# Two half-height matmuls side by side in TensorE's rows: the second passes of a 64-row tile in a GEGLU layer's gate and up

## The chip, the cores and the metric

The kernel runs on one core of one Trainium2 chip. The metric is the device time of one execution in microseconds, the median over several runs. The matrix engine (TensorE, PE in the profile) multiplies a stationary operand, loaded into its array of 128 rows by 128 columns by a weight load (PEld), with a moving operand, and adds the result to a bank of PSUM. VectorE is DVE, ScalarE is ACT, GpSimd is POOL, SyncE is SP.

## The reference

All arrays are float32; S = 2048 tokens, D = 448, F = 1792.

```python
def ref(x, dft_seq_re, dft_seq_im, dft_hid_re, dft_hid_im, w_gate, w_up, w_down):
    xn = layernorm(x)                                  # 2048 x 448, no scale or shift
    a, b = xn @ dft_hid_re.T, xn @ dft_hid_im.T        # Fourier transform over the hidden axis
    s = dft_seq_re @ a - dft_seq_im @ b                # and over the tokens, real part
    g = silu((gelu(xn @ w_gate) * (xn @ w_up)) @ w_down)
    return x + s * g
```

The change concerns `xn @ w_gate` and `xn @ w_up`, together 2048 x 448 by 448 x 3584.

## The kernel before, in words

**Precision.** Each float32 operand is split into a high part (rounded to the type fp32r of the matrix engine, by ScalarE) and a low part (the rest, by VectorE). A product is three passes over the array: high by high, high by low and low by high; low by low is left out. `three` (line 468) issues these.

**The stages.** After layernorm, transposes and the first two tiles of F in the ordinary way (`gu_mm`, line 394), 24 units of gate and up in seven products follow (function `strassen`, line 480), six groups of four, from about 72 to 397 us. Then come the hidden transform (`hid_mm`, line 985) and the transform over the tokens, also in seven products (lines 1174 and 1177).

**One unit** takes one tile of F (128 columns of gate and 128 of up) and one pair of token blocks (512 tokens each, c and e). Gate and up for both blocks are a 2 x 2 block product, made from seven products with sums of the operands by Winograd's scheme. The contraction of 448 is cut into four tiles of 128, 128, 128 and 64 rows; two by two these are the halves of the inner axis, so each of the seven products has two tiles. Four PSUM banks x1 to x4 hold the results. Sums of the weights are made by GpSimd (`sums_s`), sums of the tokens by `combine`, once; `t` and `v` are the token sums split into high and low, `hl(c, k)` the plain tokens.

**The tile of 64 rows.** Tokens of that tile are stored twice, in rows 0 to 63 and again in rows 64 to 127. Three weight tiles, x4, x2 and x3 (the first 384 columns of a weight slot), meet it. They hold the high part of the 64 weight rows in rows 0 to 63 and the low part in rows 64 to 127; line 360 makes that low part. So one pass over 128 rows adds high by high and low by high together, and a second pass with the tokens' low part adds high by low (and low by low). `two` (line 475, matmuls at line 478) issues these two passes, three times a unit: for x1, for x3 and for x4.

**The order.** It is written out by hand: the program order of each engine is the order of the calls in `strassen`, with four slots `dn` (each issues one output tile of the down product, six matmuls at line 448, and its copy out of PSUM by ScalarE, line 455) and four slots `preps` (weights of a later unit: line 354 on ScalarE, lines 356 and 360 on VectorE). `late` is the end of the unit before. Around the change the order on TensorE is: a12 and x2 into x1, a22 and x3 into x3, a down tile, s4 and x4 into x4, a down tile. ScalarE takes the gelu of x1 (line 519), VectorE adds x3 (line 523) and multiplies (line 524), ScalarE makes the high part of the result (line 526) and VectorE the low one (line 528).

Of the kernel before, what the change touches and what calls it, by code (L numbers as in the profile page):

```python
# [8 lines left out]
F32 = mybir.dt.float32  # L9
FR = mybir.dt.float32r  # L10
AF = mybir.ActivationFunctionType
ALU = mybir.AluOpType

P = 128
# [31 lines left out]
def fnet_geglu(ctx: ExitStack, tc: tile.TileContext, x, ca, ct, cp, et, wgu, wd, out):  # L46
# [13 lines left out]
    nc = tc.nc  # L60
# [31 lines left out]
    def tmp(i):  # L92
        return a_t[:, 512 * i : 512 * i + 512]
# [7 lines left out]
    def xk(c, k, lo=0):  # L101
        at = k if c % 2 == 0 else (0, 2, 1, 3)[k]
        return a_x[c][:, 2048 * lo + 512 * at :][:, :512]
# [17 lines left out]
    def bank(i, name):  # L121
        return psum.tile([P, 512], F32, name=name, tag=f"b{i}")
# [12 lines left out]
    def mm_tile(name):  # L135
        return in_turn("mm", name)
# [165 lines left out]
    def slot(i):  # L302
        return a_w[:, 3200 * i :][:, :3200]
# [43 lines left out]
    def prep_s(i, raw):  # L347

        w = slot(i)
        hw = w[:, :1792]  # L350
        steps = []

        def part_(a, b):
            nc.scalar.activation(hw[:, a:b], raw[:, P + a : P + b], AF.Copy)  # L354
            lo = max(a, 384)
            nc.vector.tensor_sub(  # L356
                w[:, 1408 + lo : 1408 + b], raw[:, P + lo : P + b], hw[:, lo:b].bitcast(F32)
            )
            if a == 0:
                nc.vector.tensor_sub(  # L360
                    hw[64:, :384], raw[64:, P : P + 384], hw[64:, :384].bitcast(F32)
                )

        names = "x4 x2 x3 s1 a11 a12 a22 b11 r1 s3 s2 s4 r3 r2".split()
        parts = {}
        for n, name in enumerate(names):
            parts[name] = [w[:, n * P : (n + 1) * P]]
            if n > 2:
                parts[name].append(w[:, 1408 + n * P : 1408 + (n + 1) * P])
        return parts, [lambda: part_(0, 896), lambda: part_(896, 1792)]  # L370
# [38 lines left out]
    def new_hs(f, c):  # L409
        hs_of[f, c] = hs_tile()  # L410
        return hs_of[f, c]
# [56 lines left out]
    def three(ps, a, b, first=False):  # L468

        for n, (i, j) in enumerate(((0, 0), (0, 1), (1, 0))):  # L470
            nc.tensor.matmul(  # L471
                ps, a[i], b[j], start=first and n == 0, stop=n == 2, skip_group_check=True
            )

    def two(ps, a, b):

        for xt in b:
            nc.tensor.matmul(ps, a[0], xt, start=False, stop=True, skip_group_check=True)  # L478

    def strassen(f, p, w, late, dn, preps):  # L480


        c, e = 2 * p, 2 * p + 1
        m, u, g1, c21 = [tmp(i) for i in ((0, 1, 2, 3), (2, 3, 0, 1))[units_n[0] % 2]]
        units_n[0] += 1

        def hl(c, k):
            return xk(c, k), xk(c, k, 1)

        t, v = t_hl[p]  # L490

        def bank(i):
            return mm_tile(f"x{i}_{f}_{p}")

        x1 = bank(1)
        three(x1, w["a11"], hl(c, 0), True)
        three(x1, w["b11"], hl(c, 2))
        nc.scalar.activation(m, x1, AF.Copy)
        late[0]()
        x2 = bank(2)  # L500
        three(x2, w["s2"], t[1], True)
        three(x2, w["r2"], v[1])
        nc.vector.tensor_add(u, m, x2)
        late[1]()
        dn[0]()
        preps[0]()
        x3 = bank(3)
        three(x3, w["s3"], t[2], True)
        three(x3, w["r3"], v[2])
        nc.vector.tensor_add(m, u, x3)  # L510
        x4 = bank(4)
        three(x4, w["s1"], t[0], True)
        three(x4, w["r1"], v[0])
        nc.vector.tensor_add(m, m, x4)
        preps[1]()
        dn[1]()
        three(x1, w["a12"], hl(c, 1))
        two(x1, w["x2"], hl(c, 3))
        nc.scalar.activation(g1, x1, AF.Gelu_apprx_tanh)
        preps[2]()  # L520
        three(x3, w["a22"], t[3])
        two(x3, w["x3"], v[3])
        nc.vector.tensor_add(c21, u, x3)
        nc.vector.tensor_mul(g1, g1, c21)  # L524
        hs = new_hs(f, c)
        nc.scalar.activation(hs[:, 0], g1, AF.Copy)  # L526
        dn[2]()
        nc.vector.tensor_sub(hs[:, 1], g1, hs[:, 0])
        preps[3]()
        three(x4, w["s4"], hl(e, 1))  # L530
        two(x4, w["x4"], hl(e, 3))
        nc.vector.tensor_add(u, u, x4)
        nc.scalar.activation(u, u, AF.Gelu_apprx_tanh)
        dn[3]()

        def late0():
            nc.vector.tensor_mul(u, u, m)
            late0.hs = new_hs(f, e)
            nc.scalar.activation(late0.hs[:, 0], u, AF.Copy)

        def late1():
            nc.vector.tensor_sub(late0.hs[:, 1], u, late0.hs[:, 0])

        return late0, late1
# [4 lines left out]
    with tc.manual_schedule():  # L549
# [294 lines left out]
        for gi in range(1, len(GROUPS)):  # L844
# [7 lines left out]
            for bi, (i, p) in enumerate(zip((0, 1, 1, 0), sides)):  # L852
# [63 lines left out]
                if gi == 1 and bi < 2:  # L916
                    dn = [nop, send, nop, send]
                run = [lambda q=q: [f() for f in q] for q in preps]
                late = strassen(grp[i], p, ws[i], late, dn, run)
                sum_step(4 * gi + bi - 4)  # L920
                if bi % 2:
# [52 lines left out]
        def hid_mm(k):  # L974
            c, kk = divmod(k, 4)
            sl = slice(kk * P, (kk + 1) * P)
            ps = []
            for r in range(2):
                p = (mm_tile if k < 2 else in_turn8)(f"ab{k}_{r}")
                xh, xl = [[xk(c, b, lo)[:, sl] for b in range(4)] for lo in range(2)]  # L980
                mm = [(xh[b], e_at[b][r]) for b in range(4)]
                mm += [(xh[b], e_at[b][2 + r]) for b in range(3)]
                mm += [(xl[b], e_at[b][r]) for b in range(4)]
                for n, (a, b) in enumerate(mm):
                    nc.tensor.matmul(p[:, :D], a, b, start=n == 0, stop=n == len(mm) - 1)  # L985
                ps.append(p[:, :D])
            return ps
# [101 lines left out]
        for k in [*range(14), 15, 14]:  # L1089
            ps = hid_mm(k)  # L1090
# [24 lines left out]
            for c, at, v in ((2, 3, (a_st, 0)), (3, 4, None), (0, 4, None), (1, 5, (a_st, 1))):  # L1115
                if k == at:
                    v, i = v or (x0, int(c == 0))
# [145 lines left out]
        def gather(ps):  # L1263

            p = {q: v[:, :D].rearrange("p (w d) -> p w d", w=2) for q, v in ps.items()}
            c11, c12, c21, c22 = [cv[t][:, :, s] for t in range(2) for s in range(2)]
            nc.scalar.activation(c11, p[1], AF.Copy)
            return [
                lambda: nc.vector.tensor_sub(c12, c11, p[6]),
                lambda: nc.vector.tensor_add(c11, c11, p[2]),  # L1270
                lambda: nc.vector.tensor_add(c21, c12, p[7]),
                lambda: nc.vector.tensor_sub(c12, c12, p[5]),
                lambda: nc.vector.tensor_sub(c22, p[5], c21),
                lambda: nc.vector.tensor_add(c12, c12, p[3]),
                lambda: nc.vector.tensor_sub(c21, p[4], c21),
            ]
# [15 lines left out]
        for m, (j, k) in enumerate(units):  # L1292
            u = m % UN
            if u == 0:
                ps = {q: bank(banks[i], f"p{q}_{j}") for i, q in enumerate(PRODUCTS)}
            if u < NS:
                if j < NK // 2 - 1 or u < NS - 2:
                    seven(m, ps)
                for i, at in enumerate(LOAD_AT if j < NK // 2 - 1 else LAST_AT):
# [5 lines left out]
                    a, b = [v.rearrange("p (b d) -> p b d", d=D) for v in (TS[n], td[n])]  # L1305
                    a, b = a[:, PARTS[h]], b[:, PARTS[h]]
# [13 lines left out]
            elif u == NS - 1:  # L1320
                todo = gather(ps)
# [10 lines left out]
            elif u == NS + 1:  # L1332
                prep_c(m + 3)
                c = cs[1][0]
# [75 lines left out]
```

## Time and profile before

| | |
|---|---|
| time, median of 3 runs | 769.71 us (769.7 to 770.01) |
| profiled execution | 769.68 us |
| its span, first to last instruction | 767.8 us |
| TensorE busy, matmuls / weight loads | 761.8 / 686.6 us (99% / 89% of the span) |
| VectorE / ScalarE / GpSimd busy | 544.8 / 366.2 / 180.1 us |
| matmuls in all | 4054 |
| granted TensorE clock | 1.00 |

Times are microseconds unless marked ns. A row of the profile names the line of the program, the engine, the operation, what it writes and reads (out<-in, buffer numbers left out, so x1 to x4 are all "x"), the shape, and for TensorE the part of the array that it uses (128*128). Matmuls are pipelined and their ends are modelled: one lasts longer than the distance to its successor's start. The chain of waits is followed back from the last instruction; the chain in order of time gives each piece the time until the next piece starts. L12 is line 12.

### The profile page before, as it was taken

The numbers are of one execution on the slowest core, as the hardware profiler recorded it, in microseconds if no ns is written. First come the engines' busy times: TensorE is split into PE (matmuls) and PEld (weight loads), VectorE is DVE, ScalarE is ACT, GpSimd is POOL, SyncE is SP. The second block draws the span as 40 slices with busy tenths as digits, with TensorE's granted clock in tenths as the row PEclk, the third lists the DMA queues.
The fourth block names the chain that finished last, engine by engine and source line by source line (L and its number), as shares of the span: only waits on it lengthen the run. The fifth ranks groups of instructions, "written<-read, shape, count | busy, mean of one in ns | idle before, by whom it ended". The sixth has DMA issues, their size and how long they took to land.

```text
span 767.8 us, 11360 instructions
## 1 busy us (share of the span) xinstructions
PE 761.8 (99%) x4054; PEld 686.6 (89%) x4054; DVE 544.8 (71%) x947; ACT 366.2 (48%) x546; POOL 180.1 (23%) x303
## 2 busy tenths in 40 slices
PE   8999999999999999999999999999999999999998
PEld 7988888888888888888889999999999999999997
DVE  7889877555556556456452776888888797979787
ACT  5875554444444344344444585544444444434341
POOL 2204043430501512501011001223232322323130
PEclk9999999999999999999999999999999999999999
DMA  8234458994959968875979981959696969788794
GB/s 297 91 120 150 145 203 176 258 186 105 266 105 254 269 117 221 176 156 86 260 215 244 371 340 54 311 181 333 216 355 191 355 205 333 222 301 264 260 299 166
DMA packets 61513, 170.04 MB, mean 221 GB/s; under 512 B 7440, under 2 KB 40080, under 8 KB 60560
## 3 DMA queue, kind: packets, MB, share of 16 engines
q0 software_dynamic: 13728, 61.02, 35.0%
q1 hardware_dynamic: 34272, 82.48, 30.5%
q10 hardware_dynamic: 13456, 25.81, 9.2%
q8 instruction: 32, 0.52, 0.3%
q14 instruction: 25, 0.20, 0.1%
HBM read 127.21 MB, written 70.91 MB: 258 GB/s over the span
## 4 chain that ended last, share of the span: by engine, by line
PE 98%; DVE 1%; issue 0%; ACT 0%; DVEq 0%
PE x L471 24%; PE p L1174 22%; PE po L448 18%; PE p L1177 10%; PE ab L985 9%; PE x L478 4%; PE gu L394 4%; PE py L1189 1%; PE py L1191 1%; PE py L1190 1%; PE gu L597 1%; PE pt L198 1%; PE warm L571 1%; PE p L1207 0%; DVE st L155 0%
## 5 line engine op out<-in xcount | busy, mean ns | idle before, releaser
L471 PE MATMUL x<-xt,w 128*128 128x512 f32 x480 | 149.4, 392 | 0.0
L471 PEld LDWEIGHTS x<-xt,w 128*128 128x128 f32 x480 | 90.1, 188 | 16.1 <-DVE tmp L510 0.4
L455 ACT ACTIVATE po_out<-po 128x448 f32<-128x448 f32 x112 | 60.2, 537 | 81.6 <-PE po L448 80.0
L448 PE MATMUL po<-wd0h,hs 128*128 128x448 f32 x256 | 81.7, 366 | 0.0
L460 POOL DMA_DIRECT2D gs<-po_out x24 | 21.4, 893 | 218.8 <-ACT po_out L455 218.7
L985 PE MATMUL ab<-e,xt 128*128 128x448 f32 x288 | 68.8, 365 | 0.0
L448 PE MATMUL po<-wd,hs 128*128 128x448 f32 x288 | 66.0, 365 | 0.0
L471 PE MATMUL x<-t_v,w 128*128 128x512 f32 x216 | 60.7, 389 | 0.0
L448 PEld LDWEIGHTS po<-wd,hs 128*128 128x128 f32 x288 | 54.1, 188 | 6.7
L985 PEld LDWEIGHTS ab<-e,xt 128*128 128x128 f32 x288 | 54.1, 188 | 4.3
L448 PEld LDWEIGHTS po<-wd0h,hs 128*128 128x128 f32 x256 | 48.1, 188 | 4.9
L471 PEld LDWEIGHTS x<-t_v,w 128*128 128x128 f32 x216 | 40.5, 188 | 8.7
L1065 POOL DMA_DIRECT2D raw<-sums x45 | 24.8, 553 | 94.9 <-DVE xt L143 55.5
L448 PE MATMUL po<-wd0l,hs 128*128 128x448 f32 x128 | 46.9, 367 | 0.0
L142 ACT ACTIVATE e<-raw 128x896 fp32r<-128x896 f32 (+1 forms) x30 | 27.7, 923 | 38.6 <-DVE raw L1072 25.8
L526 ACT ACTIVATE hs<-tmp 128x512 fp32r<-128x512 f32 x24 | 15.2, 635 | 54.6 <-DVE tmp L524 54.6
L471 PE MATMUL x<-t_lo,w 128*128 128x512 f32 x96 | 37.4, 389 | 0.0
L142 ACT ACTIVATE e<-tmp 128x896 fp32r<-128x896 f32 (+1 forms) x22 | 19.8, 898 | 35.3 <-DVE tmp L1072 26.6
L1174 PE MATMUL p<-t_v,wd0l 128*128 128x448 f32 x112 | 36.4, 374 | 0.0
L1174 PE MATMUL p<-w,e 128*128 128x448 f32 x112 | 36.4, 374 | 0.0
L1065 POOL DMA_DIRECT2D tmp<-sums x39 | 21.5, 552 | 61.2 <-DVE xt L143 38.5
L356 DVE TENSOR_TENSOR w<-raw,w 128x512 fp32r<-128x512 f32 (+1 forms) x24 | 21.3, 889 | 18.3 <-ACT w L354 18.3
(373 smaller groups left out, 2019.1 us busy)
## 6 DMA issues: line engine op xcount, KB each, us to landing
gs<-po_out POOLq DMA_DIRECT2D x24, 896.0 KB, 8.4
sums<-ca SPq DMA_DIRECT2D x16, 896.0 KB, 10.8
sums<-ca POOLq DMA_DIRECT2D x16, 896.0 KB, 14.5
t_v<-td ACTq DMA_DIRECT2D x24, 448.0 KB, 5.8
w<-td ACTq DMA_DIRECT2D x24, 448.0 KB, 8.4
raw<-ct SPq DMA_DIRECT2D x45, 192.0 KB, 4.3
raw<-wgu SPq DMA_DIRECT2D x12, 640.0 KB, 5.5
tmp<-ct SPq DMA_DIRECT2D x39, 192.0 KB, 4.7
```

The source lines that it names most:

```text
L142: nc.scalar.activation(h, src, AF.Copy)
L356: nc.vector.tensor_sub(w[:, 1408 + lo : 1408 + b], raw[:, P + lo : P + b], hw[:, lo:b].bitcast(F32))
L394: nc.tensor.matmul(ps[:, cols], a, xt[:, cols], start=n == 0, stop=n == len(mm) - 1)
L448: nc.tensor.matmul(po[:, :D], hs[:, a, kk * P : (kk + 1) * P], wdn[b][:, i], start=n == 0, stop=n == 5,)
L455: nc.scalar.activation(out_[0][:, kk], po[:, :D], AF.Copy)
L460: nc.gpsimd.dma_start(gv[:, 4 * c : 4 * c + 4], out_[0], accum_op=ALU.add)
L471: nc.tensor.matmul(ps, a[i], b[j], start=first and n == 0, stop=n == 2, skip_group_check=True)
L478: nc.tensor.matmul(ps, a[0], xt, start=False, stop=True, skip_group_check=True)
L985: nc.tensor.matmul(p[:, :D], a, b, start=n == 0, stop=n == len(mm) - 1)
L1065: nc.gpsimd.dma_start(v[:, 4 * P : 6 * P], sums[j][:, KS.index(k)])
L1174: nc.tensor.matmul(ps[q][:, :D], h, v, start=u % UN == 0, stop=False, skip_group_check=True)
L1177: nc.tensor.matmul(ps[q][:, :HD], l, v[:, :HD], start=False, stop=u % UN == NS - 1, skip_group_check=True,)
```

## The change

Three things change. In `strassen`, the `two` of x1 and that of x3 issue only their first pass. Their second passes are issued together behind x3's, by a new function `beside`: each contracts over 64 rows only, x1's in rows 0 to 63 of the array and x3's in rows 64 to 127, each to its own bank. The gelu of x1 follows the pair and, on ScalarE and in the order of the calls, comes behind `preps[2]`. So that x3's high weights lie in rows 64 to 127, the weight tile x3 has its halves swapped: the low part goes to rows 0 to 63, and one subtraction (64 x 384) becomes two (64 x 256 and 64 x 128). The product low by low, which the second passes of x1 and x3 added along the way, is no longer added there. x4 keeps both its passes.

```diff
@@ prep_s
             if a == 0:
-                nc.vector.tensor_sub(
-                    hw[64:, :384], raw[64:, P : P + 384], hw[64:, :384].bitcast(F32)
-                )
+                for r, e0, e1 in ((slice(64, P), 0, 256), (slice(0, 64), 256, 384)):
+                    nc.vector.tensor_sub(
+                        hw[r, e0:e1], raw[r, P + e0 : P + e1], hw[r, e0:e1].bitcast(F32)
+                    )
@@ behind two
+    def beside(*todo):
+        for (ps, a, b), at in zip(todo, (0, 64)):
+            r = slice(at, at + 64)
+            nc.tensor.matmul(
+                ps, a[0][r], b[1][r], start=False, stop=True, skip_group_check=True,
+                tile_position=(at, 0),
+            )
@@ strassen
         three(x1, w["a12"], hl(c, 1))
-        two(x1, w["x2"], hl(c, 3))
-        nc.scalar.activation(g1, x1, AF.Gelu_apprx_tanh)
+        two(x1, w["x2"], hl(c, 3)[:1])
         preps[2]()
         three(x3, w["a22"], t[3])
-        two(x3, w["x3"], v[3])
+        two(x3, w["x3"], v[3][:1])
+        beside((x1, w["x2"], hl(c, 3)), (x3, w["x3"], v[3]))
+        nc.scalar.activation(g1, x1, AF.Gelu_apprx_tanh)
         nc.vector.tensor_add(c21, u, x3)
         nc.vector.tensor_mul(g1, g1, c21)
```

TensorE's program order in one unit (the tile of F number 5, first pair of token blocks), from the second use of x1 to the down tile behind x3; x1 and x3 are the banks, xt0 and xt1 plain tokens of the two blocks, t_lo and t_v0 token sums, w the weights, po2 the down tile. Before:

```order
L471 MATMUL x1_5_0_1434<-xt0_66,w_73 128x512 x3
L478 MATMUL x1_5_0_1434<-xt0_66,w_73 128x512 x2
L471 MATMUL x3_5_0_1461<-xt1_67,w_73 128x512
L471 MATMUL x3_5_0_1461<-t_lo_728,w_73 128x512
L471 MATMUL x3_5_0_1461<-xt1_67,w_73 128x512
L478 MATMUL x3_5_0_1461<-t_v0_699,w_73 128x512 x2
L448 MATMUL po2_2_2_1501<-wd0h_76,hs1_80 128x448
```

And now, with the new line 487:

```order
L473 MATMUL x1_5_0_1438<-xt0_66,w_73 128x512 x3
L480 MATMUL x1_5_0_1438<-xt0_66,w_73 128x512
L473 MATMUL x3_5_0_1465<-xt1_67,w_73 128x512
L473 MATMUL x3_5_0_1465<-t_lo_729,w_73 128x512
L473 MATMUL x3_5_0_1465<-xt1_67,w_73 128x512
L480 MATMUL x3_5_0_1465<-t_v0_700,w_73 128x512
L487 MATMUL x1_5_0_1438<-xt0_66,w_73 128x512
L487 MATMUL x3_5_0_1465<-t_v0_700,w_73 128x512
L450 MATMUL po2_2_2_1505<-wd0h_76,hs1_80 128x448
```

One second pass each has gone from x1 and x3, and two matmuls of 64 rows (the row shows the output's shape, 128x512) stand ahead of the down tile.

ScalarE's order in a unit that prepares weights (tile of F number 4, second pair; po1 are down tiles, raw1 the loaded weights, w the prepared ones, tmp the working tiles). Before:

```order
L455 ACTIVATE po_out_82<-po1_2_1_1271 128x448
L519 ACTIVATE tmp_81<-x1_4_1_1225 128x512
L354 ACTIVATE w_73<-raw1_75 128x896
L526 ACTIVATE hs1_80<-tmp_81 128x512
L455 ACTIVATE po_out_82<-po1_2_2_1295 128x448
```

And now:

```order
L457 ACTIVATE po_out_82<-po1_2_1_1275 128x448
L354 ACTIVATE w_73<-raw1_75 128x896
L535 ACTIVATE tmp_81<-x1_4_1_1228 128x512
L539 ACTIVATE hs1_80<-tmp_81 128x512
L457 ACTIVATE po_out_82<-po1_2_2_1299 128x448
```

The gelu of x1 (L519, now L535) has moved behind the copy of the weights (L354).

## The prediction

> **What bounds the kernel now.** I read four views in this order: the page's busy times, its chain of waits, the engines' busy time in the stage that the change touches, and the waits of that stage.
>
> The page's sections 1 and 4 first:
>
> ```profile
> PE 761.8 (99%) x4054; PEld 686.6 (89%) x4054; DVE 544.8 (71%) x947; ACT 366.2 (48%) x546; POOL 180.1 (23%) x303
> PE 98%; DVE 1%; issue 0%; ACT 0%; DVEq 0%
> PE x L471 24%; PE p L1174 22%; PE po L448 18%; PE p L1177 10%; PE ab L985 9%; PE x L478 4%; PE gu L394 4%; PE py L1189 1%; PE py L1191 1%; PE py L1190 1%; PE gu L597 1%; PE pt L198 1%; PE warm L571 1%; PE p L1207 0%; DVE st L155 0%
> ```
>
> TensorE's matmul stream is 98% of the chain that ended last. The lines of gate and up in seven products are L471 (24%) and L478 (4%, the two passes of the 64-row tile). A page's share is an average, so the stage itself, cut in three (columns: stretch, then PE, PEld, DVE, ACT, POOL busy, granted clock, DMA share, GB/s), and its only TensorE wait:
>
> ```profile
> 70.00:180.00 110.00, 110.00 (x501) 93.74 (x500) 75.96 (x107) 50.82 (x89) 30.57 (x52) 1.00 0.70 189
> 180.00:290.00 110.00, 110.00 (x505) 94.49 (x504) 62.96 (x87) 47.28 (x83) 30.66 (x54) 1.00 0.81 193
> 290.00:397.00 107.00, 107.00 (x491) 91.92 (x491) 58.88 (x86) 47.33 (x82) 20.43 (x32) 1.00 0.78 186
> PEld x L471 <- DVE tmp L510: 0.4, 1, 0.4
> ```
>
> From 70 to 397 us TensorE never pauses, at full clock, and waits for another engine 0.4 us in all. What is taken off its stream there is taken off the time, and what is put on it is added. The other engines are idle for a third or more of the stage.
>
> The lengths of the passes come from the chain in order of time (start, length, line, instructions) in one such unit:
>
> ```profile
> 167.69 2.74 PE x L471 x12
> 170.43 1.21 PE po L448 x6
> 171.64 0.70 PE x L471 x3
> 172.34 0.46 PE x L478 x2
> 172.80 0.68 PE x L471 x3
> 173.48 0.45 PE x L478 x2
> 173.93 1.21 PE po L448 x6
> 175.14 0.70 PE x L471 x3
> 175.84 0.46 PE x L478 x2
> ```
>
> A pass over 512 columns occupies the stream 2.74/12 = 228 ns, one over 448 columns 1.21/6 = 202 ns. The difference gives 0.416 ns a column, so 213 ns for 512 columns and about 15 ns a pass that doesn't depend on the columns.
>
> **The change part by part.** The last chain shows three pairs of L478 in a unit; two of them lose their second pass. How many units there are, and how long a pass and its weight load last when they stand alone (minimum, median, maximum ns), is in the rows of L478:
>
> ```profile
> L478 PEld LDWEIGHTS x<-xt,w x96: 187/188/188, 78.9 to 396.1; 128*128 128x128 f32 x96
> L478 PE MATMUL x<-xt,w x96: 388/389/393, 79.2 to 396.3; 128*128 128x512 f32 x96
> L478 PE MATMUL x<-t_v,w x48: 389/389/397, 80.3 to 393.9; 128*128 128x512 f32 x48
> ```
>
> 96 + 48 = 144 passes, six a unit, 24 units. *Removed:* two passes a unit, 2 x 228.3 = 456.7 ns. *Added:* two matmuls of 64 rows over 512 columns. If they run side by side, they cost one pass and a second start: 228.3 + 15.4 = 243.7 ns. (The lower bound of the second start is 0, the upper one a whole pass, 228 ns, if they don't run side by side; I take the 15 ns as the only part of a pass that two instructions in different rows cannot share.) That alone is 213.0 ns a unit, 24 x 213.0 = 5.11 us: 769.68 - 5.11 = 764.6 us.
>
> *The two changes of the array's shape.* Every matmul in this trace is of shape 128*128, so what it costs to go to half-row tiles and back, 48 times, no row shows. It decides the sign: at 213 ns a unit for both, the gain is gone. From below, the nearest row is another change of what the array does, between transposes and products, early in the program:
>
> ```profile
> 33.65 0.44 PE pt L198 x4
> 34.09 1.23 PE po L448 x6
> 35.31 0.44 PE pt L198 x4
> 20.61 0.87 PE pt L198 x8
> ```
>
> Eight transposes in a row take 0.87 us, 109 ns each, so four 0.435; four between products take 0.44. Going in and out costs some 5 ns: lower bound 0. From above: a pass lasts 389 ns from start to end and the next starts after 228, so 161 ns of it lie beside its successor. If the array must have finished all of it, each change costs 161 ns, and if in addition no weight load may run ahead, its 188 ns too. With the second tile's weights loaded 109 ns behind the first's (a transposition, one weight load each, passes every 109 ns), that makes 228 + 109 + 2 x (161 + 188) = 1035 ns a unit in place of 457: +13.9 us, 783.6 us, the upper bound.
>
> The value I take stands between these. A weight load lasts 188 ns but one passes every 109, so 79 ns of it is a run-up that overlaps its predecessor. I assume the same run-up for a matmul: of the 161 ns, 79 are on the way to the array and can overlap, and 161 - 79 = 82 are in the array and behind it. Going in, the full-height pass has to leave: 82 ns. Coming out, a tile of half the rows leaves in half of that: 41 ns. Sum 123 ns a unit. It is nearer to the transposes' row than to the upper one, because only what is in the array needs its shape. Net: 213 - 123 = 90 ns a unit, 24 x 90 = 2.2 us.
>
> On this the Trainium skill speaks against the change: TensorEngine Tiling (Array Packing), Tiling Modes, says that a change of the tiling mode drains the TensorE, without a length. TensorE: Matmul & The Clock Gate, Single matmul latency, puts what a lone matmul takes beyond its columns at 398 cycles at 2.4 GHz, an estimate of 166 ns; with that at each change the sum would be 24 x (332 - 213) = +2.9 us, 772.5 us. The trace's 161 ns agrees with that figure; no row here shows a drain.
>
> *Weights' halves (L360).* One VectorE subtraction of 64x384 becomes two, 64x256 and 64x128, in 12 weight tiles. The rows:
>
> ```profile
> L360 DVE TENSOR_TENSOR w<-raw,w 64x384 fp32r<-64x384 f32 x12 | 6.7, 556 | 0.4
> L356 DVE TENSOR_TENSOR w<-raw,w 128x512 fp32r<-128x512 f32 x12 | 8.2, 686 | 0.7 <-ACT w L354 0.7
> L356 DVE TENSOR_TENSOR w<-raw,w 128x896 fp32r<-128x896 f32 x12 | 13.1, 1091 | 17.7 <-ACT w L354 17.6
> ```
>
> (1091 - 686)/384 = 1.05 ns a column and some 145 ns fixed: the second instruction adds about 0.14 us, 1.7 us in all on VectorE. It is hidden, since VectorE idles in the same unit, 1.96 us of it right behind (timeline of VectorE and ScalarE, idle time in brackets):
>
> ```profile
> 171.79 0.56 DVE L360 TENSOR_TENSOR w<-raw,w 64x384 fp32r<-64x384 f32 x1
> 172.83 0.60 ACT L519 ACTIVATE tmp<-x 128x512 f32<-128x512 f32 x1 [0.61 <-PE x L478]
> 173.33 0.94 ACT L354 ACTIVATE w<-raw 128x896 fp32r<-128x896 f32 x1
> 174.30 1.09 DVE L356 TENSOR_TENSOR w<-raw,w 128x896 fp32r<-128x896 f32 x1 [1.96 <-ACT w L354]
> 175.31 0.68 DVE L523 TENSOR_TENSOR tmp<-tmp,x 128x512 f32<-128x512 f32 x1
> ```
>
> Without that cover it would cost 1.7 us.
>
> *The gelu (L519) moves behind the pair.* Here x1 would be ready at about 173.8 instead of 172.8, and its 0.60 us end by 174.5 at the latest. Behind it on ScalarE stand the copy of L526, which needs L524 and hence L523, at 175.31 + 0.68 anyway, and before it the weight copy L354, which now goes first and is done earlier, so L356 too. TensorE needs x1's bank again in the next unit, after two products of down (1.21 us each) and five passes (1.14 us): not before 177 us. Cost 0; if the 2.5 us of slack were gone, the next unit's first pass would wait. No DMA is issued elsewhere; the first unit of each pair of token blocks waits for the copied rows of the 64-row tile as before, at the same instructions.
>
> Sum: 769.68 - 2.2 = **767.5 us**. The profiled execution (769.68, span 767.8 and 1.9 outside it) is the median of the runs (769.71) within 0.03.
>
> **The rivals.**
>
> *The pass must leave entirely (slower).* Place: both ends of each pair. Price: 161 ns each if the weights are loaded ahead, 24 x (322 - 213) = +2.6 us, 772.3 us. It decides from 107 ns a change on. For it: the 161 ns are there to be lost wherever two neighbours may not overlap. Against it: the transposes' 5 ns.
>
> *Weights cannot be loaded ahead across the change (slower).* Each change exposes at least a load of 188 ns and the second tile's comes 109 ns later: 228 + 109 + 376 - 457 = 256 ns a unit, +6.2 us, 775.8 us, and up to 783.6 us with the 161 ns. It decides from about 60 ns of exposed load a change. Against it: in the whole stage the loads (94 us of each 110) lie beside matmuls of the same rows. The Trainium skill, TensorE: Matmul & The Clock Gate, Part 3, says of tiled matmuls that a load overlaps a running matmul only where its row group is another one; by that rule this rival holds. The loads of the whole array here do overlap matmuls of the same rows, so the trace disagrees for that shape and shows nothing for tiles.
>
> *A wash.* Both changes together cost 149 to 277 ns, or the two matmuls run one after the other (228 + 228, no gain) with changes as cheap as the transposes': 769.7 us, give or take 1.5. That second way is the one in which the change doesn't do what it says; for it, no row shows any two matmuls side by side; against it, they share neither rows nor bank.
>
> **How the numbers follow.** About 0.2% (1.54 us) is what a measurement of this kernel can tell from no change. Chances: forecast (changes below 149 ns a unit) 0.42, its own range 764.6 to 768.2; wash 0.17; the pass must leave entirely 0.23; weights not loaded ahead 0.18, half of it beyond 776 us. So faster 0.42, same 0.17, slower 0.41, and the range 764.5 to 776.0 leaves out the dear half of the last rival. The time is that of the likeliest single case, though the slower ones together weigh nearly as much.
>
> **What would show it.** In the profile after, the 64-row matmuls should appear with another shape than 128*128, 48 in number, the second of each starting some 15 ns behind the first; if it starts 100 ns or more behind, the loads set it, and at 228 they don't run side by side. The chain in order of time gives the stretch between the last full pass of x3 and the first product of down behind the pair: I expect 244 + 123 = 367 ns; 244 if changes are free, 457 at the break-even, 566 if passes must leave, over 700 with exposed loads. TensorE should still have no wait above 0.4 us there, the rest of the chain its old lengths, and L523 and L526 no later against their unit's end. Wrong would be a stretch above 457 ns, or a new wait of TensorE for the gelu or the weights.

## The result, and the profile after

The changed kernel takes 774.12 us (median of 4, 773.92 to 774.23), the kernel before 769.86 (median of 4). The ratio is 1.0055, 95% interval 1.0043 to 1.0067: slower by 4.3 us, where 2.2 us faster was forecast. The time lies inside the stated range and on the other side of no change. Two single executions of runs further down had a far lower granted clock than all others (824.06 us at 0.85 with six passes held back, 1250.53 us at 0.56 with more room), and the medians below leave them out (with them, 774.96 and 768.6 us).

Where it went is in one unit. The chain in order of time of the changed kernel (start, length until the next piece, line, instructions; L480 are the full first passes, L487 the 64-row pair, L450 the down product):

```profile
172.90 0.70 PE x L473 x3
173.59 0.23 PE x L480
173.82 0.68 PE x L473 x3
174.50 0.23 PE x L480
174.73 0.43 PE x L487 x2
175.16 1.42 PE po L450 x6
```

Before, six matmuls of the down product took 1.21 us in such a unit; behind the pair they take 1.42. The pair and that excess are 0.43 + 0.21 = 0.64 us, where two full passes were 0.46. The difference, 0.18 us, times 24 units is the 4.3 us. Of the 0.64 us, 0.23 is one pass; 0.41 us is the price of going in and out.

The timelines of that place show what the price consists of. First the weight loads:

```profile
174.12 0.19 PEld L480 LDWEIGHTS x<-t_v,w 128*128 128x128 f32 x1
174.66 0.18 PEld L487 LDWEIGHTS x<-xt,w 64*128 64x128 f32 x1 [0.35 <-issue]
174.66 0.18 PEld L487 LDWEIGHTS x<-t_v,w 64*128 64x128 f32 x1
175.09 0.19 PEld L450 LDWEIGHTS po<-wd0h,hs 128*128 128x128 f32 x1 [0.24 <-issue]
175.20 0.19 PEld L450 LDWEIGHTS po<-wd0l,hs 128*128 128x128 f32 x1
```

and the matmuls:

```profile
174.34 0.39 PE L480 MATMUL x<-t_v,w 128*128 128x512 f32 x1
174.66 0.50 PE L487 MATMUL x<-xt,w 64*128 64x512 f32 x1
174.66 0.50 PE L487 MATMUL x<-t_v,w 64*128 64x512 f32 x1
175.09 0.47 PE L450 MATMUL po<-wd0h,hs 128*128 128x448 f32 x1
175.40 0.36 PE L450 MATMUL po<-wd0l,hs 128*128 128x448 f32 x1
```

Three things can be read here. The pair does run side by side: both loads start at 174.66, and so do both matmuls (their 0.50 us includes the load before them, and its end is modelled). The loads do not run ahead: the one before the pair starts 0.22 us ahead of its matmul as everywhere, but the pair's start only 0.32 us after the last full pass has started, that is 92 ns after its 228 ns are over. And the way out looks like the way in: the first load of the down product waits until 175.09, and since its second matmul starts at 175.40, its first must have occupied the array from 175.40 - 0.20 = 175.20, 0.11 us after its load began. From the end of the last full pass to there it is 630 ns, 402 more than the 228 of one pass: that is measured. If both ways cost the same, a change of shape costs about 92 ns in which nothing starts and 109 ns for a load that nothing covers, 201 ns. The third experiment below shows that they do.

Nothing else became a bound. TensorE's waits in the stage (waiting engine, what it waited for, total, times, longest):

```profile
PEld x L487 <- issue: 8.5, 24, 0.4
PEld po L450 <- issue: 5.4, 22, 0.2
PEld x L473 <- issue: 0.5, 2, 0.2
PEld x L473 <- DVE tmp L522: 0.4, 1, 0.4
```

"Issue" is a wait for which no other engine is to blame. The only wait for another engine is the 0.4 us that was there before.

### The profile page after: what moved, and what is told of

Same layout as the page of the kernel before. It is cut to its first block, busy times and chain, and to the rows that moved or that the text cites. A ratio compares the mean times of both kernels' runs of the same rounds, so it can differ in the third digit from the quotient of the medians.

```text
span 772.0 us, 11384 instructions
## 1 busy us (share of the span) xinstructions
PE 766.2 (99%) x4054; PEld 680.3 (88%) x4054; DVE 551.6 (71%) x959; ACT 367.0 (48%) x546; POOL 180.6 (23%) x303
## 4 chain that ended last, share of the span: by engine, by line
PE 99%; DVE 1%; issue 0%; ACT 0%; DVEq 0%
PE x L473 24%; PE p L1187 21%; PE po L450 18%; PE p L1190 10%; PE ab L998 9%; PE gu L396 4%; PE x L480 3%; PE py L1202 1%; PE py L1204 1%; PE py L1203 1%; PE x L487 1%; PE gu L610 1%; PE pt L198 1%; PE warm L584 1%; PE p L1220 0%; DVE st L155 0%
## 5 line engine op out<-in xcount | busy, mean ns | idle before, releaser
L450 PE MATMUL po<-wd0h,hs 128*128 128x448 f32 x256 | 82.8, 371 | 0.0
L450 PE MATMUL po<-wd,hs 128*128 128x448 f32 x288 | 67.4, 369 | 0.0
L450 PEld LDWEIGHTS po<-wd,hs 128*128 128x128 f32 x288 | 53.2, 188 | 8.7 <-issue 2.9
L450 PEld LDWEIGHTS po<-wd0h,hs 128*128 128x128 f32 x256 | 48.1, 188 | 6.9 <-issue 2.4
L450 PE MATMUL po<-wd0l,hs 128*128 128x448 f32 x128 | 46.9, 366 | 0.0
L515 DVE TENSOR_TENSOR tmp<-tmp,x 128x512 f32<-128x512 f32 x24 | 16.5, 687 | 30.8 <-PE x L473 30.4
L143 DVE TENSOR_TENSOR e<-raw,e 128x896 fp32r<-128x896 f32 (+1 forms) x30 | 31.4, 1046 | 3.7 <-ACT e L142 3.4
```

Of the source, the lines that this page charges most:

```text
L143: nc.vector.tensor_sub(l, src, h)
L450: nc.tensor.matmul(po[:, :D], hs[:, a, kk * P : (kk + 1) * P], wdn[b][:, i], start=n == 0, stop=n == 5,)
```

## The experiments

### Is it the shape, or the order?

Both second passes stay where the change put them, but run over all 128 rows.

```diff
-        beside((x1, w["x2"], hl(c, 3)), (x3, w["x3"], v[3]))
+        two(x1, w["x2"], hl(c, 3)[1:])
+        two(x3, w["x3"], v[3][1:])
```

> The order of the change (second passes of x1 and x3 together behind x3, gelu behind them, weight halves swapped, two subtractions), but both second passes over all 128 rows, so no change of the array's shape. Theory A (the loss is the two changes of shape, about 400 ns a unit beyond the passes): the time of before, 769.5 to 770.3 us. Theory B (part of the loss comes from the moved gelu, the longer VectorE work or the new order): clearly above, 771 us or more, with a wait of TensorE or ScalarE that before does not have.

Measured: 770.3 us against 769.78 in the same session, ratio 1.0006, interval 0.9997 to 1.0015. The interval includes no change, and the time is at the upper edge of what theory A expected. In its profile the three adjoining passes cost what they should:

```profile
173.91 0.68 PE x L480 x3
174.59 1.21 PE po L450 x6
```

The half microsecond is there in the profile too. TensorE waits longer for a sum of VectorE than before (0.4 us, once), and the stage ends 0.66 us later, at 398.54 in place of 397.88:

```profile
PEld x L473 <- DVE tmp L522: 1.2, 3, 0.7
```

So the moved gelu, the swapped halves and the second subtraction cost some half a microsecond here, 1.2 us at the upper end of the interval; why that wait grew is not shown. The changed kernel has it at 0.4 us as before, so its 4.3 us lie at the 64-row shape.

### Does one lone 64-row pass cost the same?

```diff
-        beside((x1, w["x2"], hl(c, 3)), (x3, w["x3"], v[3]))
+        beside((x1, w["x2"], hl(c, 3)))
+        two(x3, w["x3"], v[3][1:])
```

> Only x1's second pass over 64 rows, alone, and x3's second pass over 128 rows behind it. Theory A (a fixed price for going in and out, about 400 ns, whatever runs between): 24 x 0.40 = +9.6 us on before, 779 to 780 us. Theory B (the price comes from two tiles at once, by their loads, rows or banks): a lone 64-row pass costs little more than a full one, 770 to 774 us.

Measured: 779.12 us, ratio 1.0122 (1.0107 to 1.0137), 9.3 us above before, 0.39 us a unit. Its chain in order of time has the lone pass and, behind it, a full pass with the price of the way out:

```profile
175.72 0.23 PE x L480
175.95 0.43 PE x L487
176.38 0.43 PE x L480
176.80 1.21 PE po L450 x6
```

The lone tile takes the 0.43 us of the pair, and the full pass behind it 0.43 in place of 0.23. So the second tile of a pair costs nothing, and the price doesn't come from having two tiles. Theory A stands.

### Is the price for the change, or for each pass?

```diff
         beside((x1, w["x2"], hl(c, 3)), (x3, w["x3"], v[3]))
+        beside((x1, w["x2"], hl(c, 3)), (x3, w["x3"], v[3]))
```

> The pair is issued twice in a row (the two low parts are added twice, which is no longer the layer's result). Theory A (the price is for the change of shape alone; within the half-row shape passes follow each other as elsewhere): one pass more a unit, 24 x 0.228 = +5.5 us on the changed kernel, 779.3 to 780.0 us. Theory B (within the half-row shape no weight load runs ahead): 109 to 188 ns more for each further pair, 782 to 784.5 us. If the tiles did not run side by side: +10.9 us, 785 us.

Measured: 779.55 us, ratio 1.0129 (1.0112 to 1.0146), 5.4 us above the changed kernel (5.5 if each is taken against before in its own session) or 0.226 us a unit, one ordinary pass. The weight loads in its timeline:

```profile
175.94 0.18 PEld L487 LDWEIGHTS x<-xt,w 64*128 64x128 f32 x1 [0.35 <-issue]
175.94 0.18 PEld L487 LDWEIGHTS x<-t_v,w 64*128 64x128 f32 x1
176.05 0.19 PEld L487 LDWEIGHTS x<-xt,w 64*128 64x128 f32 x1
176.05 0.19 PEld L487 LDWEIGHTS x<-t_v,w 64*128 64x128 f32 x1
176.60 0.19 PEld L450 LDWEIGHTS po<-wd0h,hs 128*128 128x128 f32 x1 [0.36 <-issue]
```

and the matmuls of one of the two tiles:

```profile
175.62 0.39 PE L480 MATMUL x<-t_v,w 128*128 128x512 f32 x1
175.94 0.49 PE L487 MATMUL x<-xt,w 64*128 64x512 f32 x1
176.28 0.39 PE L487 MATMUL x<-xt,w 64*128 64x512 f32 x1
```

The second pair's loads start 0.11 us behind the first's, while the first pair is still at work in the same rows (the second pair's matmuls start at 176.28). Within the half-row shape loads run ahead as they do in the full shape; only the first after a change is held back. The Trainium skill, TensorE: Matmul & The Clock Gate, Part 3, says in its list of what overlaps that a load does so only where the row group differs. This trace doesn't agree: the loads at 176.05 lie beside the first pair's matmuls in the same rows.

The rows also part the way in from the way out. The second pair follows the first after 0.34 us, a pass of 0.23 and 0.11 more, so the first pair's columns began 0.11 us after its load: the exposed load of the way in. The down product's load starts 0.32 us behind the second pair, 0.09 after its 0.23 are over: the pause of the way out, as long as that of the way in (175.62 to 175.94). The Trainium skill, TensorEngine Tiling (Array Packing), Tiling Modes, says that a change of mode drains the engine. This trace agrees, if the pause of 92 ns is that drain.

### Can the price be shared?

A visit to the half-row shape costs 402 ns and then 228 ns a pair. Three pairs in one visit cost 3 x 228 + 402 = 1086 ns and replace six full passes, 1370 ns. So all six second passes of two units have to be issued together. The banks allow it: down keeps two, the two units have six, and x4 takes the bank of x2. In one of the two weight slots the halves are swapped, so that each pair has one operand from each slot. The results stay in PSUM until the end of the second unit, and the element-wise work of both units follows at once. Nine of the twelve pairs of units were built so; the first group and the last pair of units keep full passes.

```diff
...
+        beside((p1, w0["x2"], hl(c, 3)), (q1, w1["x2"], hl(c, 3)))
+        beside((p4, w0["x4"], hl(e, 3)), (q4, w1["x4"], hl(e, 3)))
+        beside((q3, w1["x3"], v[3]), (p3, w0["x3"], v[3]))
+        for n in range(2):
+            nc.scalar.activation(g[n], ps1[n], AF.Gelu_apprx_tanh)
+            nc.vector.tensor_add(ps3[n], us[n], ps3[n])
+            nc.vector.tensor_add(us[n], us[n], ps4[n])
...
```

(p1, p3, p4 are x1, x3, x4 of the unit whose weights are in the first slot, q1, q3, q4 those of the other.)

> The price of the shape change shared by six second passes: in nine of the twelve pairs of units all six of both units (x1, x3, x4 twice) are held back and issued as three pairs of 64-row matmuls behind the second unit; the other six units keep full passes. Theory A (about 402 ns for going in and out, 228 ns a pair): 3 x 228 + 402 = 1086 ns in place of 6 x 228 = 1370 ns, 0.28 us a pair of units, 9 x 0.28 = 2.6 us less than before: 766.8 to 767.6 us. Rival: the element-wise work of two units now comes at once behind the pairs, and TensorE waits for its banks or for the down product's operands: 769 us or more, with a wait of TensorE for VectorE or ScalarE in the stage.

And the control, in the same order with full passes:

```diff
-        beside((p1, w0["x2"], hl(c, 3)), (q1, w1["x2"], hl(c, 3)))
-        beside((p4, w0["x4"], hl(e, 3)), (q4, w1["x4"], hl(e, 3)))
-        beside((q3, w1["x3"], v[3]), (p3, w0["x3"], v[3]))
+        for ps, a, b in (...):        # the same six, in the same order
+            two(ps, a, b[1:])
```

> The same order as the run with six held back, but the six second passes over all 128 rows. If the order of the two units costs nothing: the time of before, 769.5 to 770.5 us, and 2.6 us above the run with 64-row pairs. If the burst of element-wise work makes TensorE wait, both are later by that wait, and the difference between them stays 2.6 us.

Measured: 774.4 us (ratio 1.0064, 1.0044 to 1.0084) with pairs and 775.2 (1.0066, 1.0051 to 1.0081) with full passes. Both are slower than before, and theory A missed. The rival was right about the burst. The first one's waits:

```profile
PEld po L453 <- DVE hs L577: 3.0, 5, 0.7
PEld x L476 <- DVE tmp L514: 1.3, 4, 0.4
PEld x L476 <- DVE tmp L522: 0.8, 2, 0.4
PEld po L453 <- ACT hs L576: 0.6, 1, 0.6
```

The down product waited for its operands (L577), and x4 and x3 waited for the sums that free or read their banks (L514, L522). The two medians, 0.8 us apart, do not show the 2.6 us between them: the three executions with pairs scattered from 771.8 to 775.5, and the profile is of the fastest. The two profiled executions are further apart (spans of 770.0 and 773.1 us), but this pair of runs alone settles nothing.

### With room for the burst

The first unit's x2 takes a bank of the second unit, which is free until then, so x4 no longer waits for it. The first unit's down tiles come one product later, and the high and low parts of the second token block behind the unit's own sums.

```diff
-        x2 = bank(b0 + 1, f"x2_{f}_{p}")
+        x2 = bank(4 if last else 3, f"x2_{f}_{p}")
...
-        late[2]()
-        if not last:
-            dn[0]()
         x4 = bank(b0 + 1, f"x4_{f}_{p}")
         three(x4, w["s1"], t[0], True)
         three(x4, w["r1"], v[0])
         nc.vector.tensor_add(m, m, x4)
+        if not last:
+            dn[0]()
+        late[2]()
...
```

> Six second passes of two units as three pairs of 64-row matmuls again, with more room for the element-wise work: the first unit's x2 gets a bank that is free until the second unit, its down tiles come one product later, and the high and low parts of the second token block are made after the unit's own sums. Theory A (402 ns a visit to the half-row shape): 9 x 0.28 = 2.6 us under the kernel before, 766.8 to 767.6 us, with at most 1 us of TensorE waits in the stage. Rival (the burst of work behind the pairs cannot be covered): waits of 3 us or more remain, 770 us or more.

> The order of the run with more room, its six held-back second passes over all 128 rows. Theory A: 9 x 0.28 = 2.6 us above that run (768.6 us), 770.8 to 771.6 us, and so within 2 us above before: what is gained there comes from the 64-row pairs and not from the new order. Rival (the new order itself gained): 768.6 us or less.

Measured: 768.5 us with pairs (769.96 before in that session; ratio 0.9984, 0.9974 to 0.9994), and 771.17 with full passes (769.96 before in its session too; ratio 1.0018, 1.0009 to 1.0028). The difference is 2.6 us, as 9 x 0.28 says. In the chain in order of time of the run with pairs, three pairs in one visit:

```profile
146.17 0.23 PE x L483
146.39 0.89 PE x L489 x5
147.28 2.63 PE po L453 x12
```

0.89 us, and 2.63 for twelve matmuls of down, which take 2 x 1.21 = 2.42 elsewhere: 0.89 + 0.21 = 1.10 us in place of 1.37 (the chain lists five of the six matmuls; the timeline has all six). This version beats both kernels, by 0.16% and 0.7%, though it lies a microsecond above what was expected of it: the control shows that its order costs about 1.2 us against before. TensorE's waits for other engines in the stage, with pairs and then in the control, account for it:

```profile
PEld po L453 <- DVE hs L581: 1.0, 1, 1.0
PEld x L476 <- DVE tmp L618: 0.4, 1, 0.4
PEld po L453 <- DVE hs L584: 1.2, 1, 1.2
PEld x L476 <- DVE tmp L621: 0.5, 1, 0.5
```

In the control they are 1.7 us, where before had 0.4: 1.3 us more. With pairs they are 1.4 us, so of the 2.6 us a microsecond goes into one wait of the down product.

## Why the prediction was wrong

**The bound: right.** The stream of TensorE sets the stage, and what the pair costs more than two passes came out on the time one to one: 0.18 us x 24 = 4.3 us.

**Side by side: right.** The two 64-row matmuls start together, not 15 ns apart, and so do their loads; the lone tile in the second experiment costs what the pair costs. The rival in which they run one after the other is refuted.

**What is free: nearly right.** The first experiment carries the moved gelu, the swapped halves and the longer subtraction; its interval includes no change, and its profile puts some half a microsecond on them. The changed kernel has no new wait of TensorE. The two subtractions of the changed kernel take 423 + 283 ns in place of 556, 0.15 us more, where 0.14 was forecast:

```profile
L362 DVE TENSOR_TENSOR w<-raw,w 64x256 fp32r<-64x256 f32 x11 | 4.6, 423 | 0.3
L362 DVE TENSOR_TENSOR w<-raw,w 64x128 fp32r<-64x128 f32 x11 | 3.1, 283 | 0.1
```

**The step that failed: "Sum 123 ns a unit", the price of the two changes of shape.** It measured 402 ns, and 213 was the break-even. The way in, 82 ns for a pass to leave, was nearly right as a pause: 92 ns. The way out, 41 ns because a tile of half the rows leaves in half the time, was wrong: in the third experiment the pause behind the 64-row pair is 92 ns as well, and a lone tile is followed by the same excess as a pair. And the forecast let the weight loads run ahead across the change; they don't, and each change exposes 109 ns of one, the distance at which loads pass each other, not the 188 ns that one lasts. The choice rested on the nearest row, transposes between products at 5 ns. That row shows another operation in the same 128*128 shape and says nothing of a change of shape. It was also read short: behind the transposes the six matmuls of down took 1.23 us in place of 1.21, some 20 ns that the 5 leave out.

**The rivals.** "The pass must leave entirely" put 161 ns on each change, with loads ahead: wrong mechanism, since the tail of a pass is not waited for in full (92 ns of the 161), and loads don't run ahead. "Weights cannot be loaded ahead across the change" was the right one, with a chance of 0.18, and mis-sized: it charged 188 ns a load and another 109 for the second tile, +6.2 us; the two loads run at once, a load is worth 109, and the pause comes on top: 2 x (92 + 109) + 228 - 457 = 173 ns a unit, 4.2 us. Its sentence on loads lying beside matmuls of the same rows was true and beside the point, since they do so within a shape, in both shapes.

**The stretch.** From the pair to the first matmul of down 367 ns were forecast, over 700 for exposed loads; it was about 630.

## What to carry to other kernels

Two half-height matmuls side by side are worth one pass saved, but every visit to the half-row shape had a fixed price here, 402 ns against 228 ns for a pass of 512 columns. One pair a visit therefore lost and three pairs a visit won. Other shapes and types were not measured. So count the visits, not the pairs, and collect the half-height work of several steps in one visit as far as the PSUM banks reach; then look at what the held-back results do to the engines behind, since in this kernel the burst cost more than the gain until its order was mended.

## What was not expected of the hardware

Between the shapes 128*128 and 64*128, the first weight load in the new shape does not start until about 92 ns after the 228 ns of the last pass in the old one are over, and 109 ns of it are then exposed; this holds both ways (174.66 us in the changed kernel, 176.60 in the third experiment), and a lone tile pays as much as a pair (0.43 us and 0.20 behind it in the second experiment). Two tiles' loads, in different rows, run at the same time (both at 174.66 us), as do their matmuls. Within the half-row shape a load runs ahead beside a matmul in the same rows (176.05, its own matmul at 176.28), as in the full shape (174.12 and 174.34).
